# Decode attention on one core: explicit semaphores, hardware loops on TensorE, and A's loads ahead of B's

## The chip, the cores and the metric

The kernel runs on one core of one Trainium2 chip. Times are device microseconds (us) of that core, as medians of several executions. On a single core the runs carry no visible slow state; all runs compared here were marked "fast", and their times lie within about 0.4% of each other for any one kernel. A change counts as faster or slower when it moves the time by over 2%.

Names of engines in profile lines: PE is TensorE (PEld its weight loads), DVE VectorE, ACT ScalarE, POOL GpSimd, and SPq the SyncE queue that issues the DMAs. The page counts 16 DMA engines for the core.

## The reference, cut to what matters

Two single-token decode attentions, A and B, each with 32 heads of 128. A reads 16384 keys and values per head, B only the last 4096. Weights `wq` and `wo` are 4.2 MB each, for each problem.

```python
q = (x @ wq).reshape(B, Sq, Hq, Dh)                      # one token
scores = einsum("bhqd,bhkd->bhqk", q, k) * Dh ** -0.5
o = einsum("bhqk,bhkd->bhqd", softmax(scores), v)
out = o.reshape(B, Sq, Hq * Dh) @ wo
# A: k, v = k_cache, v_cache;  B: the last 4096 keys of each head;  result: concat(A, B)
```

K and V alone are 335.5 MB (A 2 x 134.2 MB, B 2 x 33.6 MB). Everything is read from HBM once (the page: 352.32 MB read).

## The kernel before

K and V come in 20 "loads" (16 of A, 4 of B) of 256 keys on each of 128 partitions: 8.39 MB for k and as much for v. There are two buffers for k (`kt`) and one for v (`vt`). For each load, VectorE multiplies k by q, adds the two halves of the 128 columns, TensorE sums the remaining 64 columns into PSUM (32 matmuls against an identity, the "bank sums"), VectorE reduces the last 8 values, ScalarE takes the exponential, and TensorE multiplies by v ("p.v", 64 matmuls). VectorE then picks the useful quarter of the result, and TensorE folds it into the heads' sums. An A load is one unit of two heads. A B load is two units of four heads, each with its own two halves of the DMA.

The main loop, written for a framework that places the semaphores itself:

```python
loads = []                                  # A A A A B  A A A A B ...
per = len(stA.loads) // len(stB.loads)
for i, x in enumerate(stA.loads):
    loads.append(x)
    if i % per == per - 1:
        loads.append(stB.loads[i // per])
...
for i, x in enumerate(loads):
    n = KEYS // (4, 2)[i] if i < 2 else KEYS
    for k in range(0, KEYS, n):
        _mult(nc, cx, x, k, k + n)                 # DVE, k *= q
        if prev is not None and k == 0:
            _softmax(nc, cx, prev)                 # DVE reduce, ACT exp
        _add(nc, cx, x, k, k + n)                  # DVE
        if prev is not None and k == 0:
            for u in prev.units:
                _pv(nc, cx, u)                     # PE, frees the v buffer
        _red(nc, cx, x, k, k + n)                  # PE bank sums, frees a k buffer
    if prev is not None:
        end(prev)                                  # DVE pick, PE fold
    prev = x
```

All of it is unrolled: TensorE's program has more than 4,000 instructions (the page counts 2148 matmuls and 2148 weight loads). The DMA queue gets k(i+1), then v(i), then k(i+2), and so on; v(i) may be issued when p.v of load i-1 is done, and k(i+2) when the bank sums of load i are done.

The softmax here doesn't subtract the row's maximum and nothing guards it: scores larger than these inputs give would overflow.

## Time and profile before

| | before |
|---|---|
| time, median | 823.2 us |
| span in the profile | 821.2 us |
| data moved by the main queue | 352.33 MB |
| busy share of that queue | 99.3% |
| DVE / PE / ACT busy | 73% / 37% / 4% |

From the page of the kernel before: two rows of the 40 equal slices of the span (busy tenths of the DMA engines, and what they moved), and the table of DMA queues (packets, MB, share of the 16 engines' time).

```profile
DMA  9999999999999999999999999999999999999997
GB/s 383 434 457 412 456 412 454 412 454 418 427 442 444 425 441 429 441 416 447 421 445 437 431 435 434 432 423 443 441 418 451 425 445 421 448 413 455 413 424 317
q1 hardware_dynamic: 8212, 352.33, 99.3%
q8 instruction: 16, 0.26, 0.1%
```

The DMA engines are busy in every slice. The swing between 412 and 457 GB/s is only a matter of counting: packets count where they start, and in a slice (20.5 us) an engine starts 8 or 9 packets of 64 KB (2.42 us each). Neighbouring slices average about 434. q8 is the fetching of TensorE's own program, 16 blocks of 16 KB.

One steady period, from the timeline of the kernel before (start us, us, engine, line, operation, result and operands, count, and in brackets the idle time before and what ended it):

```profile
294.62 17.23 DVE L169 TENSOR_TENSOR kt<-kt,qallA 128x32768 bf16<-128x32768 bf16 x1 [9.23 <-DMA kt<-in_A_k_cache_dram]
...
313.96 8.68 DVE L178 TENSOR_TENSOR kt<-kt 128x16384 bf16<-128x16384 bf16 x1
...
315.23 5.97 PE L231 MATMUL acc<-vt,p_sb 128*8 128x512 bf16 x64 [23.70 <-ACT p_sb L212]
...
321.25 0.53 SPq L158 DMA_DIRECT2D vt<-in_A_v_cache_dram  x1
...
322.70 7.08 PE L190 MATMUL red<-kt,ident 128*128 128x512 bf16 x32 [1.51 <-DVE kt L178]
...
329.71 0.41 PE L259 MATMUL f_ps<-s,selA 128*32 128x128 f32 x2
329.81 1.18 SPq L158 DMA_DIRECT2D kt<-in_B_k_cache_dram  x2
333.27 17.23 DVE L169 TENSOR_TENSOR kt<-kt,qallA 128x32768 bf16<-128x32768 bf16 x1 [9.29 <-DMA kt<-in_A_k_cache_dram]
```

Read it from the DMA queue's side. A multiply starts when its k has landed, so k loads land at 294.6 and 333.3, 38.7 us apart. The next v load was handed to the queue at 321.25, 12 us before the k load ahead of it was done. That "lead" is what keeps the queue from running empty.

The end of the span, from the same kernel's timeline:

```profile
815.69 1.04 PE L307 MATMUL out_ps<-wo_t,ocB 128*1 128x256 bf16 x16 [0.43 <-DMA wo_t<-in_B_wo_dram]
...
816.91 1.00 PE L307 MATMUL out_ps<-wo_t,ocB 128*1 128x256 bf16 x12 [0.18 <-DMA wo_t<-in_B_wo_dram]
...
818.21 0.38 PE L307 MATMUL out_ps<-wo_t,ocB 128*1 128x256 bf16 x4 [0.29 <-DMA wo_t<-in_B_wo_dram]
```

TensorE waits for each of the last pieces of B's `wo`, but only for 0.2 to 0.4 us.

### The profile page before, as it was taken

How to read it: one execution, taken by the hardware profiler on the slowest of the kernel's cores; microseconds unless marked ns; L12 is line 12 of the kernel's file. 1: busy time of each engine (PE TensorE's matmuls, PEld its weight loads, DVE VectorE, ACT ScalarE, POOL GpSimd, SP SyncE). 2: the span in 40 equal slices, each digit the busy share in tenths (PEclk: the TensorE clock that was granted, in tenths of full speed). 3: DMA queues.
4: the chain of work that ended last, by engine and by line, in shares of the span. 5: the costliest groups of instructions: out<-in, count | busy, mean ns of one | idle time of the engine just before them, and what ended most of it. 6: DMA issues, size and time to landing. Idle time of an engine off the chain costs nothing.

```text
span 821.2 us, 4767 instructions
## 1 busy us (share of the span) xinstructions
PE 301.1 (37%) x2148; PEld 117.3 (14%) x2148; DVE 600.7 (73%) x146; ACT 35.1 (4%) x133; POOL 1.3 (0%) x9
## 2 busy tenths in 40 slices
PE   3433705143223415060606151423414250606076
PEld 1111202011011102020202020101101020202033
DVE  2099895997496867799196949599659677689921
ACT  0100000000010000000001000000001000000010
POOL 0000000000000000000000000000000000000000
PEclk9855668586767677675858585857666676768599
DMA  9999999999999999999999999999999999999997
GB/s 383 434 457 412 456 412 454 412 454 418 427 442 444 425 441 429 441 416 447 421 445 437 431 435 434 432 423 443 441 418 451 425 445 421 448 413 455 413 424 317
DMA packets 8235, 352.62 MB, mean 429 GB/s; under 512 B 916, under 2 KB 920, under 8 KB 1304
## 3 DMA queue, kind: packets, MB, share of 16 engines
q1 hardware_dynamic: 8212, 352.33, 99.3%
q8 instruction: 16, 0.26, 0.1%
q14 instruction: 3, 0.02, 0.0%
q10 hardware_dynamic: 4, 0.00, 0.0%
HBM read 352.32 MB, written 0.00 MB: 429 GB/s over the span
## 4 chain that ended last, share of the span: by engine, by line
DMA 61%; issue 15%; DVE 13%; PE 11%; ACT 0%; SPq 0%; DVEq 0%
DMA kt<-in_A_k_cache_dram 42%; DMA vt<-in_A_v_cache_dram 12%; PE red L190 7%; DVE kt L178 6%; DVE kt L169 4%; PE acc L231 4%; DMA vt<-in_B_v_cache_dram 4%; DMA wo_t<-in_B_wo_dram 4%; DVE sc L206 2%; ACT p_sb L212 0%; SPq L115 0%; PE out_ps L307 0%; DVE rowB L316 0%; DVEq L169 0%
## 5 line engine op out<-in xcount | busy, mean ns | idle before, releaser
L169 DVE TENSOR_TENSOR kt<-kt,qallA 128x32768 bf16<-128x32768 bf16 (+2 forms) x20 | 276.2, 13810 | 162.5 <-DMA kt<-in_A_k_cache_dram 162.5
L231 PE MATMUL acc<-vt,p_sb 128*8 128x512 bf16 (+1 forms) x1280 | 113.0, 530 | 444.4 <-ACT p_sb L212 344.4
L178 DVE TENSOR_TENSOR kt<-kt 128x16384 bf16<-128x16384 bf16 (+2 forms) x24 | 174.3, 7261 | 0.2
L190 PE MATMUL red<-kt,ident 128*128 128x512 bf16 x640 | 151.2, 396 | 54.6 <-DVE kt L178 54.6
L231 PEld LDWEIGHTS <-p_sb 128*8 128x8 bf16 (+1 forms) x1280 | 37.6, 112 | 515.7 <-ACT p_sb L212 419.8
L190 PEld LDWEIGHTS <-ident 128*128 128x128 bf16 x640 | 63.0, 101 | 142.2 <-issue 47.1
L169 DVE TENSOR_TENSOR kt<-kt,qallB 128x16384 bf16<-128x16384 bf16 x8 | 69.5, 8686 | 2.9 <-DMA kt<-in_B_k_cache_dram 2.9
L206 DVE TENSOR_REDUCE sc<-red 128x256 f32<-128x2048 f32 x20 | 45.7, 2284 | 5.6 <-PE red L190 5.6
L212 ACT ACTIVATE p_sb<-sc,offA 128x256 bf16<-128x256 f32 x32 | 16.0, 500 | 574.7 <-DVE sc L206 574.7
L245 DVE TENSOR_TENSOR acc<-acc,maskA 128x512 f32<-128x512 f32 x16 | 11.1, 694 | 21.4 <-PE acc L231 21.4
L212 ACT ACTIVATE p_sb<-sc,offB 128x128 bf16<-128x128 f32 x32 | 12.4, 388 | 161.2 <-DVE sc L206 161.2
L130 PE MATMUL q_ps<-wq_t,scr 128*128 128x512 bf16 x64 | 15.7, 407 | 6.9 <-DMA wq_t<-in_A_wq_dram 4.9
L251 DVE TENSOR_REDUCE s<-acc 128x128 f32<-128x512 f32 x24 | 16.6, 691 | 0.8
L307 PE MATMUL out_ps<-wo_t,ocA 128*1 128x512 bf16 x32 | 8.8, 443 | 0.3 <-DVE ocA L300 0.3
L245 DVE TENSOR_TENSOR acc<-acc,maskB 128x512 f32<-128x512 f32 x8 | 5.5, 692 | 4.5 <-PE acc L231 4.5
L130 PEld LDWEIGHTS <-scr 128*128 128x128 bf16 x64 | 6.5, 103 | 15.6 <-issue 8.0
L316 DVE CAST rowA<-out_ps 1x512 bf16<-1x512 f32 x1 | 0.7, 678 | 8.8 <-PE out_ps L307 8.8
L259 PE MATMUL f_ps<-s,selA 128*32 128x128 f32 x32 | 6.5, 285 | 0.0
L212 ACT ACTIVATION_READ_ACCUMULATOR p_sb<-sc,offA 128x1 f32 x32 | 6.0, 187 | 0.0
L212 ACT ACTIVATION_READ_ACCUMULATOR p_sb<-sc,offB 128x1 f32 x32 | 6.0, 186 | 0.0
L307 PE MATMUL out_ps<-wo_t,ocB 128*1 128x256 bf16 x64 | 4.3, 272 | 1.8 <-DMA wo_t<-in_B_wo_dram 0.9
L102 DVE CAST scr<-xT 128x128 bf16<-128x128 f32 (+1 forms) x6 | 2.1, 459 | 3.6 <-PE xT L94 3.5
(43 smaller groups left out, 26.4 us busy)
## 6 DMA issues: line engine op xcount, KB each, us to landing
kt<-in_B_k_cache_dram SPq DMA_DIRECT2D x8, 4096.0 KB, 32.4
vt<-in_B_v_cache_dram SPq DMA_DIRECT2D x8, 4096.0 KB, 23.8
wq_t<-in_A_wq_dram SPq DMA_DIRECT2D x1, 4096.0 KB, 12.2
wq_t<-in_B_wq_dram SPq DMA_DIRECT2D x1, 4096.0 KB
wo_t<-in_A_wo_dram SPq DMA_DIRECT2D x2, 2048.0 KB, 22.6
wo_t<-in_B_wo_dram SPq DMA_DIRECT2D x1, 2048.0 KB, 27.0
wo_t<-in_B_wo_dram SPq DMA_DIRECT2D x1, 1024.0 KB, 29.0
wo_t<-in_B_wo_dram SPq DMA_DIRECT2D x1, 512.0 KB
```

The lines of the kernel that those rows point to most:

```text
L102: cx.o(nc.vector.tensor_copy(st.xb[:, :, g, :].rearrange("p c (i r) -> p r c i", r=R)[:, g, :, :], xT[:, :].rearrange("p (c o) -> p c o", ...
L130: cx.o(nc.tensor.matmul(q_ps[:, j, :], lhsT=st.xb[:, c, g, :], rhs=w[:, g, j * (512 // DH) : (j + 1) * (512 // DH), :], start=(g == 0 and ...
L169: cx.o(nc.vector.tensor_tensor(out=k, in0=k, in1=q.rearrange("p (o d) -> p o d", o=1).broadcast_to([P, b - a, DH]), op=ALU.mult,))
L178: cx.o(nc.vector.tensor_tensor(out=k[:, :, 0 : DH // 2], in0=k[:, :, 0 : DH // 2], in1=k[:, :, DH // 2 : DH], op=ALU.add,))
L190: cx.o(nc.tensor.matmul(load.red[:, k : k + n, :], lhsT=cx.ident[:, :], rhs=load.kt[:, k : k + n, b * W : (b + 1) * W], start=(b == 0), st ...
L206: cx.o(nc.vector.tensor_reduce(out=sc[:, :], in_=load.red[:, :, :], axis=AX.X, op=ALU.add))
L212: cx.o(nc.scalar.activation(out=u.p[:, :, g, :], in_=sc[:, u.k0 : u.k0 + n].rearrange("p (t e) -> p t e", e=4), func=ACT.Exp, scale=SCALE, ...
L231: cx.o(nc.tensor.matmul(u.acc[r : r + 4 * R, :], lhsT=u.p[:, t, :, :], rhs=u.load.vt[:, k : k + 4, :], start=(t < 4), stop=(t >= T - 4),))
L245: cx.o(nc.vector.tensor_tensor(out=acc, in0=acc, in1=st.mask[:, :].rearrange("p (x o) -> p x o", o=1).broadcast_to([P, 4, DH]), op=ALU.mult,))
L251: cx.o(nc.vector.tensor_reduce(out=u.s[:, :], in_=acc.rearrange("p x d -> p d x"), axis=AX.X, op=ALU.add,))
L259: cx.o(nc.tensor.matmul(cx.f_ps[st.f_at : st.f_at + 32, 0:DH], lhsT=st.sel[:, at : at + 32], rhs=u.s[:, :], start=(u.i == 0), stop=(u.i == ...
L307: cx.o(nc.tensor.matmul(out[x], lhsT=st.oc[:, j : j + 1], rhs=st.wo_t[:, j, x * w : (x + 1) * w], start=(j == 0), stop=(j == J - 1),))
```

## The change

Its intent: replace the framework's automatic synchronisation by semaphores set by hand, so that TensorE can run two hardware loops (16 turns over A's loads, 3 over B's, one load left over), each with an inner loop over the four PSUM banks of the sums. A loop over one kind of load needs A's loads in a row, so all of A precedes B. The order on TensorE becomes sums(i), p.v(i), fold(i), sums(i+1): the fold, which waits for VectorE's pick, now stands ahead of the next sums. Before, it came after them. The core of the diff:

```diff
-    loads = []
-    per = len(stA.loads) // len(stB.loads)
-    ...                                          # A A A A B
+    loads = [stA] * stA.L + [stB] * stB.L
...
+    def take(self, eng, n=1):                    # class _Sem
+        eng.wait_ge(self.h, n)
+        eng.sem_inc(self.h, -n)
...
+    def red(slot):
+        with e.Fori(0, NB) as n:
+            cx.s_add.take(e)
+            for b in range(W):
+                ins = mm(
+                    cx.red[:, bass.ds(n, 1), :], lhsT=cx.ident[:, :],
+                    rhs=banks[:, bass.ds(slot * NB + n, 1), :, b * W : (b + 1) * W],
+                    start=(b == 0), stop=(b == W - 1),
+                )
+            ins.then_inc(cx.s_red.h, 1)
+    def pv(st, vt, sems):
+        for u in range(st.U):
+            cx.s_p.take(e)
+            sems[u].take(e, 16)
+            ...                                  # the matmuls, unrolled as before
+            ins.then_inc(cx.s_pv.h, 1)
+        for u in range(st.U):
+            cx.s_pick.take(e)
+            ins = mm(cx.f[...], lhsT=cx.win[u][:, :], rhs=cx.s[u][:, :], start=False, stop=True)
...
+    loop = lambda a, b: nc.Fori(a, b, engines=cx.pe_only, head_slot={PE: 0})
+    with loop(1, 1 + stA.L) as i:
+        red(i % 2)
+        pv(stA, cx.vt, cx.s_v)
+    norm(stA)
+    with loop(1 + stA.L, len(loads)) as i:
+        red(i % 2)
+        pv(stB, cx.vt, cx.s_v)
+    red(n % 2)
+    pv(stB, cx.kt[:, _slot(n - 2), :, :], cx.s_vlast)
+    norm(stB)
```

The DMA queue's program keeps the same transfers in the same pattern (k ahead, v behind), each behind a hand-written wait on `s_red` or `s_pv`.

## The prediction

> What bounds the kernel now: the DMA queue. On the page, the data queue moved 352.33 MB and was busy 99.3% of the 821.2 us span, and the DMA row of the slices shows 9 in all but the last. The table by stretch of time shows 431 to 435 GB/s in every stretch from 42 to 785 us. [...] DVE is busy 73%, PE 37%, ACT 4%.
>
> Steady period of one A load, from the timeline at 294.6 to 333.3 us: 38.7 us for 16.8 MB. In it DVE works 17.2 (multiply) + 2.3 (reduce) + 8.7 (add) + 1.4 (pick) = 29.6 us; PE works 6.0 (p.v) + 7.1 (bank sums) + 0.4 (fold). The next v load is issued when p.v ends (321.25), 12 us before the k load ahead of it in the queue has landed (333.3). The k load after that is issued when the bank sums end (329.8), over 20 us before its turn. So compute can slip 12 us per load before the queue runs dry.
>
> What the change does:
> - Order on PE: the fold of load i now precedes the bank sums of i+1, which therefore wait for the pick: from 322.7 to about 324.7, 2 us later. Slack 20 us: worth 0.
> - Loops: register work, branches, explicit waits. [...] inside the slack: 0.
> - Instruction fetch: 0.26 MB now; perhaps 0.2 MB goes, 0.5 us at 429 GB/s.
> - A before B: same bytes, same transfers. DVE per B load is 17.4 + 2.3 + 8.7 + 2.8 = 31 us, below 38.7, so B loads in a row stay DMA-bound.
> - Start: the first k load lands at 42 us, q is ready at about 32; 10 us to spare. [...]
> - Tail: the last weight piece lands at 818.2; PE waits 0.2 to 0.4 us for each of the last pieces, so has about 1.3 us to spare. The load before the last is now a B load of two units, so its p.v ends near 781 instead of 785.3, which pays for the later pick[...]. End still set by DMA: 0 to +2 us.
>
> Sum: nothing of size lies on the critical path. I predict 822.5 us (before 823.2), range 819.0 to 826.5; faster by over 2%: 0.01, within 2%: 0.96, slower by over 2%: 0.03.
>
> What would show it: data queue still about 99% busy at 428 to 431 GB/s; instruction-queue bytes below 0.1 MB; bank sums starting about 2 us after the adds end; v loads issued over 8 us before the k load ahead lands; last p.v done before 803; last step of the chain a weight-load DMA, then under 1 us of PE.
>
> What would make it wrong: [...] a gap in the queue from the new k-load waits; B loads in a row streaming at another rate than A's.

The forecast came to 822.5 us, 0.7 below the 823.2 before. Terms of it are cut here, because nothing measured stood behind them: an allowance per load for the loops, counted as 0 and again hidden in the tail, and up to 1 us for entering the explicit section. The terms left are -0.5 us for the instruction bytes and 0 to +2 us at the tail.

## The result, and the profile after

| | before | after |
|---|---|---|
| time, median | 823.2 us | 822.4 us |
| span in the profile | 821.2 us | 820.4 us |
| instruction blocks for TensorE | 16 (0.26 MB) | 4 (0.07 MB) |
| bank sums, busy in total | 151.2 us | 183.3 us |
| main queue's busy share | 99.3% | 99.3% |

The ratio is 0.9987, with a 95% interval of 0.997 to 1.0005. Ratios here and below are the mean time of one kernel's runs over that of the other's of the same rounds, so they are not quite the ratio of the medians quoted.

The same lines of the page, kernel after:

```profile
DMA  9999999999999999999999999999999999999997
q1 hardware_dynamic: 8212, 352.33, 99.3%
q8 instruction: 4, 0.07, 0.0%
```

One steady period of the kernel after, from its timeline:

```profile
294.82 17.23 DVE L292 TENSOR_TENSOR kt<-kt,qallA 128x32768 bf16<-128x32768 bf16 x1 [9.23 <-DMA kt<-in_A_k_cache_dram]
...
314.16 8.68 DVE L300 TENSOR_TENSOR kt<-kt 128x16384 bf16<-128x16384 bf16 x1
...
315.67 5.89 PE L364 MATMUL acc<-vt,p 128*8 128x512 bf16 x64 [20.39 <-PEq L42]
321.60 0.53 SPq L150 DMA_DIRECT2D vt<-in_A_v_cache_dram  x1
...
323.57 0.69 DVE L327 TENSOR_REDUCE s<-acc 128x128 f32<-128x512 f32 x1
324.41 0.60 PE L364 MATMUL f<-s,win 128*32 128x128 f32 x2 [2.85 <-PEq L42]
325.58 9.50 PE L364 MATMUL red<-kt,ident 128*128 x32 [0.57 <-PEq L42]
333.42 17.23 DVE L292 TENSOR_TENSOR kt<-kt,qallA 128x32768 bf16<-128x32768 bf16 x1 [9.15 <-DMA kt<-in_A_k_cache_dram]
335.12 0.54 SPq L150 DMA_DIRECT2D kt<-in_A_k_cache_dram  x1
```

The fold now stands ahead of the sums. The sums begin 2.7 us after the add ends (at 322.8) and take 9.5 instead of 7.1 us, so the next k load is issued 5.3 us later (335.1 against 329.8). And yet the k loads land 38.6 us apart, as before: the v load is still handed over 11.8 us ahead of its turn, and the k load issued at 335.1 stands behind a v transfer that has only just begun. "PEq L42" names the wait instruction in the helper; it is TensorE's own sequencer waiting on a semaphore.

The end of the kernel after:

```profile
815.87 1.01 PE L364 MATMUL red<-vt,ocB 128*1 128x256 bf16 x12 [0.15 <-DMA vt<-in_B_wo_dram]
817.13 0.38 PE L364 MATMUL red<-vt,ocB 128*1 128x256 bf16 x4 [0.25 <-DMA vt<-in_B_wo_dram]
```

DMA still ends last, but only 0.4 us of waiting are left in these lines.

A warning on the chain of waits: the page's chain of the kernel before spread its time over many DMAs, engines and lines; that of the kernel after covers only the last 4% of the span.

```profile
DMA 4%; PE 0%; SPq 0%; DVE 0%; issue 0%
```

It starts at 778.4 us. A chain this short says nothing about the 95% in front of it; the DMA rows and the lead do.

### The profile page after: what moved, and what is told of

Same layout as the page of the kernel before. It is cut to its first block, busy times and chain, and to the rows that moved or that the text cites. A ratio compares the mean times of both kernels' runs of the same rounds, so it can differ in the third digit from the quotient of the medians. Undisturbed runs are those within 1.5% of the kernel's fastest.

```text
span 820.4 us, 5948 instructions
## 1 busy us (share of the span) xinstructions
PE 338.6 (41%) x2149; PEld 128.4 (16%) x2149; DVE 603.5 (74%) x172; ACT 35.5 (4%) x134; POOL 1.3 (0%) x9
## 3 DMA queue, kind: packets, MB, share of 16 engines
q1 hardware_dynamic: 8212, 352.33, 99.3%
## 5 line engine op out<-in xcount | busy, mean ns | idle before, releaser
L292 DVE TENSOR_TENSOR kt<-kt,qallA 128x32768 bf16<-128x32768 bf16 (+2 forms) x20 | 276.2, 13810 | 155.8 <-DMA kt<-in_A_k_cache_dram 155.8
L364 PE MATMUL acc<-vt,p 128*8 128x512 bf16 (+1 forms) x1216 | 111.1, 543 | 353.4 <-PEq L42 353.4
L364 PE MATMUL red<-kt,ident 128*128 x640 | 183.3, 456 | 43.3 <-PEq L42 43.3
L364 PEld LDWEIGHTS acc<-vt,p 128*8 128x8 bf16 (+1 forms) x1216 | 36.8, 113 | 427.1 <-issue 419.3
L364 PEld LDWEIGHTS red<-kt,ident 128*128 128x128 bf16 x640 | 72.5, 113 | 150.4 <-issue 103.7
L216 ACT ACTIVATE p<-sc,offA 128x256 bf16<-128x256 f32 x32 | 16.0, 500 | 604.9 <-DVE sc L306 604.9
L364 PE MATMUL f<-s,win 128*32 128x128 f32 x48 | 11.0, 317 | 61.4 <-PEq L42 61.4
L364 PE MATMUL red<-vt,kt 128*128 128x512 bf16 x64 | 15.6, 406 | 8.0 <-DMA vt<-in_A_wq_dram 5.9
L216 ACT ACTIVATE p<-sc,offB 128x128 bf16<-128x128 f32 x32 | 12.4, 388 | 115.7 <-DVE sc L306 115.7
L327 DVE TENSOR_REDUCE s<-acc 128x128 f32<-128x512 f32 x24 | 16.6, 692 | 0.8
L364 PEld LDWEIGHTS red<-vt,kt 128*128 128x128 bf16 x64 | 6.5, 103 | 16.7 <-issue 10.4
L364 PE MATMUL red<-vt,ocA 128*1 128x512 bf16 x32 | 8.5, 433 | 0.0
## 6 DMA issues: line engine op xcount, KB each, us to landing
vt<-in_B_wo_dram SPq DMA_DIRECT2D x1, 2048.0 KB, 29.6
```

What stands on the lines that cost most here:

```text
L216: ins = e.activation(out=p[:, :, g, :], in_=cx.sc[:, u * st.keys : (u + 1) * st.keys].rearrange("p (t e) -> p t e", e=4), func=ACT.Exp, sc ...
L292: n = did(e.tensor_tensor(out=k, in0=k, in1=q.rearrange("p (o d) -> p o d", o=1).broadcast_to([P, b - a, DH]), op=ALU.mult,))
L327: cx.s_pick.on(e.tensor_reduce(out=cx.s[u][:, :], in_=acc.rearrange("p x d -> p d x"), axis=AX.X, op=ALU.add,))
L364: mm = lambda *a, **k: e.matmul(*a, skip_group_check=True, **k)
```

## The experiments

The theory: the DMA queue sets the time; compute has about 12 us of lead per load and next to none at the end; what differs between the kernels is the instruction traffic and the two ends. Rivals are stated with each run.

### The three parts of the change, one at a time

`before_a_first` is the kernel before with only the order changed. `unrolled` is the kernel after with TensorE's loops written out. `after_again` is the kernel after itself. The three ran on one chip, five rounds each.

```diff
 # before_a_first
-    loads = []
-    ...
+    loads = stA.loads + stB.loads
 # unrolled
-        with e.Fori(0, NB) as n:
+        for n in range(NB):
-    with loop(1, 1 + stA.L) as i:
+    for i in range(1, 1 + stA.L):
-    with loop(1 + stA.L, len(loads)) as i:
+    for i in range(1 + stA.L, len(loads)):
```

> The changed kernel unaltered, for a tight interval beside the other two of this call. Theory (queue-bound, only 0.19 MB of instruction bytes and the two ends differ): 0.5 to 1.3 us faster than before, ratio 0.9985 to 0.9995. Rival (nothing differs, the 0.8 us is scatter between chips): ratio 1.000 within 0.0005.

> The changed kernel with the tensor engine's loops written out: explicit semaphores and A before B stay, hardware loops go. Theory: instruction bytes return to about 0.26 MB, the 32 bank sums of a load return from 9.5 to about 7.1 us, the next k load is issued 2 to 3 us earlier, and the time rises by the instruction bytes alone, about 0.5 us, so about 822.8. Rival 1 (loop overhead costs time): faster than the changed kernel by more than 1 us. Rival 2 (the gain comes from explicit semaphores or the order, not the loops): same as the changed kernel within 0.2 us.

> The kernel before with one edit, all of A's loads ahead of B's. Theory: same bytes through a full queue, so the time is that of before within 0.4 us (ratio 0.9995 to 1.0005); the product of p and v of the load before the last ends about 4 us earlier, hidden. Rival (order is what moved the end 1 us earlier): about 822.2, ratio 0.9985 to 0.999.

| kernel | order | semaphores | loops | median us (lowest to highest) | ratio to before |
|---|---|---|---|---|---|
| before | A A A A B | automatic | no | 823.21 (822.87 to 823.55) | 1 |
| before_a_first | A first | automatic | no | 823.31 (822.94 to 823.66) | 1.0001 |
| unrolled | A first | explicit | no | 824.93 (824.45 to 824.99) | 1.002 |
| after_again | A first | explicit | yes | 822.63 (822.39 to 822.88) | 0.9993 |

The order alone is worth nothing (+0.1 us). The rewrite with explicit semaphores, still unrolled, costs 1.6 us. The loops give 2.3 us back. So the small net change is two opposite changes, each larger than the sum, and my expectation of 0.5 us for the loops was too small by a factor of over four. The net gain itself (0.6 us here, 0.8 us in the first measurement) is as expected, and the ranges of the two kernels overlap by 0.01 us at most; but the intervals of both ratios include 1, so by them a gain of zero isn't ruled out.

In the unrolled kernel's timeline around 325 us the sums take 8.5 us against 7.1 before and 9.5 after:

```profile
324.41 0.59 PE L364 MATMUL f<-s,win 128*32 128x128 f32 x2 [2.49 <-PEq L42]
324.93 8.51 PE L364 MATMUL red<-kt,ident 128*128 128x512 bf16 x32
```

Their total of busy time over the run is 171.5 us against 151.2 and 183.3. So most of what the sums got slower (20 of 32 us) came without any loop. The pause ahead of them is longer too (2.5 us before the fold, against 1.5 us before), but no run changed the pause by itself, so it is not shown to be the reason. What the traces do show is a lower clock. The view by windows over just these 32 matmuls (tile `ident`), for the kernels before, unrolled and after; the third number from the right is the granted clock:

```profile
322.70:329.78 7.08, 7.08 (x32) 3.05 (x32) 0.00 (x0) 0.00 (x0) 1.00 1.02 444
324.93:333.44 8.51, 8.51 (x32) 3.39 (x32) 0.00 (x0) 0.00 (x0) 0.83 0.96 416
325.58:335.08 9.50, 9.50 (x32) 3.73 (x32) 0.00 (x0) 0.00 (x0) 0.74 1.02 442
```

Time multiplied by clock is 7.0 to 7.1 us in all three. In these groups a matmul starts either 0.43 or 0.22 us after the one ahead of it. In the traces of the kernels before and after, all 208 steps of 0.40 to 0.45 us fall where the record of the granted clock stands at 0.5, and all 985 of 0.20 to 0.23 us where it stands at 1.0. Over the whole run 39, 136 and 191 of the 640 sums have the slow step, and at 0.21 us each that is the 20 and the 12 us. So the loops' 12 us, too, are accounted for by these slow steps, a lower clock and not slower issue. None of this reached the time: the kernel with the slowest sums is the fastest of the four.

Where do 2.3 us come from, then? The page of the unrolled kernel:

```profile
q1 hardware_dynamic: 8212, 352.33, 99.1%
q8 instruction: 17, 0.28, 0.1%
```

Thirteen more blocks of 16 KB are 0.21 MB, or 0.5 us at 432 GB/s (the kernel before moved 431 to 435 from 42 to 785 us). The bytes don't explain it. The packets in the trace do better. Worked out from the start and length of every packet of 2 KB or more on the main queue: the last moment (us, looked at every 0.1 us) at which at least n packets were in flight on the 16 engines.

```
                blocks fetched   n=16    n=12    n=8     n=4     n=2     n=1
after                 4          814.8   814.9   815.2   816.3   816.6   816.7
before               16          814.7   815.2   817.5   817.7   817.8   817.8
before_a_first       16          814.6   814.9   817.5   817.6   817.7   818.0
unrolled             17          814.9   815.2   817.7   817.9   818.3   819.1
```

(A 17th block of `before_a_first` came at 822.6 us, after the end of the span.)

In all four kernels some engines run out of work at about 815 us. In those that fetch 16 or 17 blocks, eight packets are still in flight at 817.5 us; in the kernel after, the last of all ends at 816.7. In the trace a block's own packet takes about 0.94 us (mean), while a 64 KB data packet takes 2.42 us. The reading that fits: a fetch takes the place of data on one engine, fetches fall on half of the engines, and the time is that of the last engine, not of the mean. The next two runs put this to the test.

### More instruction blocks

`pv_x2` (below) runs p.v twice in a small hardware loop and takes 822.34 us. `pv_x2_unrolled` is the same arithmetic with every loop written out. `pool_fill` leaves TensorE as in the kernel after and gives the idle POOL engine a long useless program.

```diff
 # pv_x2_unrolled: as unrolled, and
-                with e.Fori(0, rep) as _:
+                for _ in range(rep):
                     once()
 # pool_fill, at the end of POOL's program
+    cx.s_pool.wait(e, 2)
+    for turn in range(8):
+        for i in range(1024):
+            ins = e.memset(cx.scratch[:, i : i + 1], 0)
+        cx.s_own.wait(e, cx.s_own.on(ins))
```

> pv_x2 with every tensor-engine loop written out: same arithmetic as pv_x2 (822.34 us), some 27 instead of 4 instruction blocks fetched. Theory (fetches delay single DMA engines): slower than pv_x2 by more than the 2.3 us that 13 more blocks cost the unrolled kernel, 825 to 829 us, with a wider spread of the engines' ends. Rival 1 (bytes only, 0.4 MB): 823.3. Rival 2 (unrolled code as such costs 2.3 us, whatever its length): 824.6.

> The changed kernel with 8192 useless one-column fills at the end of the otherwise idle POOL engine's program[...] while the tensor engine's loops and all data transfers stay as they are. Theory (fetches pass through the same 16 DMA engines and each delays the one that carries it by about 0.95 us, so that engines end unevenly): the last data packets of the 16 engines end over more than the 2 us of the changed kernel, 825 to 835 us. Rival 1 (only the bytes count, 0.53 MB at 432 GB/s): 823.6. Rival 2 (the unrolled kernel was slower because of the tensor engine's own timing): 822.4.

(The page below has 64 packets more on q14 than the kernel after, 0.52 MB.)

`pv_x2_unrolled`: 826.43 us (826.19 to 826.54), 27 blocks. Against `pv_x2`, measured in another call, that is 4.1 us for 23 more blocks, 0.18 us each. Against that, `unrolled` minus `after_again` is 2.3 us for 13 blocks, also 0.18 us each. A block's bytes at 432 GB/s would be 0.04 us. Its packets show the two halves again: 16 in flight until 814.6 us, 8 until 819.0, the last until 820.6. Both rivals (823.3 by bytes, 824.6 by "unrolled code as such") fell.

The kept traces show the rest of the mechanism. On one engine the next packet starts 3 or 4 ns before a 64 KB packet ends, so the packets can be chained into 16 rows, one for each engine (rows that end a packet in the same nanosecond can be swapped). In `pv_x2_unrolled` the first 16 fetches fall on eight of the rows, twice over in the same order; the other eight rows get none of them. A fetch takes 0.88 to 0.98 us, and a 64 KB packet behind it 2.9 to 3.0 instead of 2.42 us (in the kernel before 0.88 to 1.00 and 2.9 to 3.0): together about 1.4 us on its engine. Over eight engines that is 0.18 us per block, the cost that both pairs gave.

The cost comes in steps, because the last engine counts. The engines end near 815.0, 816.6, 817.8, 819.2 and 820.5 us, each step about one block's 1.4 us. With 4 blocks (`after`) four engines end on the second step. With 16 (`before`, `before_a_first`) eight end on the third. With 17 (`unrolled`) seven end on the third and one on the fourth. With 26 before 819 us (`pv_x2_unrolled`) six end on the fourth and two on the fifth. This is what blocks dealt out in turn to eight engines give. So most of the 1.6 us of "explicit semaphores" is probably the 17th block and not the waits; no run changed one without the other.

`pool_fill`: 863.97 us, ratio 1.0496, far above the 825 to 835 that I expected. Its page:

```profile
q1 hardware_dynamic: 8212, 352.33, 95.5%
q14 instruction: 67, 0.55, 0.2%
```

POOL's program came in 64 blocks of 8 KB, one every 5.5 us, and while it ran the A period was 43.9 instead of 38.7 us: 5.2 us for eight blocks, 0.65 us each, and 64 x 0.65 = 41.6 us is the whole loss. The queue's share over the whole run fell to 95.5%, and single slices to 299 GB/s. Chaining the packets as above shows why: from 228 to 353 us all 22 of POOL's fetches fall on one and the same row. Each takes 0.31 us and makes the data packet behind it 0.35 us longer, 0.66 us together. That engine has no gap in this stretch, while the other fifteen are busy for only 90 or 91% of it: every transfer waits for the one engine. The 8192 fills that POOL wrote meanwhile are a rival that no run removed, and 2 or 3 of some 46 packets on each other engine were slow as well; but those engines had time to spare. So the fetches are enough to account for the loss (0.5 MB that no one waits for cost 41 us).

### How much lead there is

`pv_x2`, `pv_x3` and `pv_x4` run every p.v but the last load's two, three and four times in a small loop. The sum restarts each time, so the result is the same. The v load is issued later, and nothing else changes.

```diff
-            for t in range(T):
-                ...
-            ins.then_inc(cx.s_pv.h, 1)
+            with e.Fori(0, rep) as _:
+                once()                           # the matmuls and their semaphore
...
-        cx.s_pv.wait(e, pv)
+        cx.s_pv.wait(e, REP * pv)
```

> Each product of p and v but the last load's is run twice (same result, restarted sum), in a small hardware loop: about 6 us more tensor-engine work per load, 115 us in all, before the next v load may be issued. Theory: an A load's period is the longer of 38.7 us (the queue) and 21.4 us (a v load on an otherwise empty queue, 19.4 plus about 2 to start and land) plus the product's own time. 21.4 + 11.8 = 33.2, so the time stays at 822 to 824; v loads are issued about 6 instead of 12 us before the k load ahead lands. Rival (work shown in the chain of waits adds up: bank sums 7%, product 4%): about 100 us slower.

The "about 2 to start and land" can be read in the kernel before: `wq` of A, the first load on an empty queue, landed 12.2 us after its issue (page, part 6), of which its 4.19 MB at 432 GB/s are 9.7; that leaves 2.5 us.

> As pv_x2, three times: 21.4 + 17.7 = 39.1 us plus loop turns, just over 38.7. Theory: the edge; 0.4 to 1.5 us on each of 16 A loads, 825 to 845 us. B loads have two units that overlap load and product, so they don't slow. Rival (the tensor engine, busy only 40%, has room to spare until it is near full): same time, 822.

> As pv_x2, four times: 21.4 + 23.6 = 45 us plus loop turns, about 6.3 to 8 us over the queue's 38.7 on each A load. Theory: 915 to 950 us, with the queue's busy share down near 88%, the tensor engine still idle a third of the time. Rival (room until the tensor engine is full; it would be about 75% busy): same time.

| kernel | median us | ratio | p.v of an A load, us | lead of v issue, us | mean A period, us | granted clock |
|---|---|---|---|---|---|---|
| after | 822.4 | 0.9987 | 4.9 to 6.5 | 11.2 to 12.9 | 38.63 | 0.695 |
| pv_x2 | 822.34 | 0.9986 | 8.4 to 9.7 | 7.9 to 10.2 | 38.68 | 0.756 |
| pv_x3 | 824.07 | 1.0002 | 11.8 to 13.3 | 4.2 to 5.8 | 38.77 | 0.798 |
| pv_x4 | 850.96 | 1.0327 | 15.4 to 16.6 | 1.4 to 3.8 | 39.66 | 0.827 |

The lead is read as in the period above: the start of the next multiply minus the issue of the v load. The period is the mean of the 13 between A's third load and its last. Adding 3 us per load costs nothing, adding 6 to 7 us little (1.7 us in all), adding 10 us breaks through. That is the slack of some 12 us, minus about 4 us which a load seems to need as a head start. In `pv_x4`, from the timelines of SPq and DVE:

```profile
380.06 0.54 SPq L151 DMA_DIRECT2D vt<-in_A_v_cache_dram  x1
```

```profile
380.89 0.69 DVE L328 TENSOR_REDUCE s<-acc 128x128 f32<-128x512 f32 x1
381.53 17.23 DVE L293 TENSOR_TENSOR kt<-kt,qallA 128x32768 bf16<-128x32768 bf16 x1
```

Here the v load was handed over only 1.5 us before the multiply of the next k began, and the queue's share over the run fell to 96.7%.

My expectations for x3 and x4 missed in size (825 to 845, 915 to 950), and for one reason: I priced each repeat at the 5.9 us of the first, and it cost 3.3. The granted clock of the run rose with the repeats, from 0.695 to 0.827, while TensorE's busy time in the stretch from 100 to 600 us rose from 202.5 to 297.3 us. In the profiled execution `pv_x4` is 29.9 us longer. Its last data packet comes 19.2 us later (835.9 against 816.7), 13 us of it in these 13 periods of 1.0 us more. The other 10.7 us are the end: after the last data packet it took 14.4 us to the end of the span (835.9 to 850.3), against 3.7 in the kernel after.

### The end of the kernel

`tail_red_x2` repeats the bank sums of the last load only.

```diff
-            for b in range(W):
+            for b in list(range(W)) * rep:
...
-    red(n % 2)
+    red(n % 2, 2)
```

> Only the bank sums of the last load are done twice (same result): about 8 us more tensor-engine work once, after the last k load. Theory: at the end the tensor engine waits for weight pieces 0.15 and 0.25 us only, so of 8 us about 0.4 to 1 is hidden: 829 to 830.5 us, and the last wait for a weight piece is gone. Rival (the end is set by the DMA with room to spare, as in the middle): 822.

It took 826.81 us (825.91 to 827.24), 4.4 us more than the kernel after and less than the 829 to 830.5 that I expected. The timeline shows how 6.8 us shrank to that: the sums went from 8.76 to 15.59 us, but the first 29 output matmuls that follow ran faster, 6.42 instead of 7.86 us, and the 0.4 us of waiting for weight pieces went too.

```profile
784.39 15.59 PE L364 MATMUL red<-kt,ident 128*128 x64
...
812.56 6.42 PE L364 MATMUL red<-vt,ocA 128*1 128x512 bf16 x29
...
819.26 3.00 PE L364 MATMUL red<-vt,ocB 128*1 128x256 bf16 x52
```

The last group has no bracket any more: TensorE no longer waits for DMA at the end. So extra TensorE work of 3 us on each of the first 19 loads was free (`pv_x2`), and on the 20th most of it was paid.

### Less vector work, fewer bytes

`thin_dve` lets the multiply and the add touch 16 of 128 columns. `half_v` moves half of each v load. Both compute something else.

```diff
 # thin_dve
-            k = cx.kt[:, _slot(i), a:b, :]
+            k = cx.kt[:, _slot(i), a:b, 0:16]
 ...                                              # q and the add likewise
 # half_v
+            if which == "v":
+                out, src = out[:, 0 : st.keys // 2, :], src[:, :, 0 : st.keys // 2, :]
```

> Wrong result on purpose: the multiply and the add of each load touch 16 of 128 columns only, so vector-engine work falls from about 600 to under 200 us while every DMA stays. Theory: queue-bound, 820 to 823 us; idle time of the vector engine grows by what it was spared. Rival (vector work on the chain of waits, 13%, counts): tens of us faster. Rival 2 (vector traffic on the on-chip memory slows the loads): steady rate rises above 435 GB/s and the time falls by over 2 us.

> Wrong result on purpose: only half of each v load is moved, 352.3 to 268.4 MB. Theory: the queue's period per load falls to about 29 us, just under the vector engine's 29.6 (A) and 31 (B), so that engine takes over: 38.7 falls to about 30 per load, 820 to about 650 us (640 to 670), vector engine about 92% busy, queue no longer full. Rival (bytes alone): 268.4 MB at 432 GB/s plus the ends, 628 us.

`thin_dve`: 822.47 us, ratio 0.9988. Removing 446 us of the vector engine's 603 us changed nothing. What the multiply no longer does, the engine waits:

```profile
L292 DVE TENSOR_TENSOR kt<-kt,qallA 128x4096 bf16<-128x4096 bf16 (+2 forms) x20 | 37.3, 1864 | 217.4 <-DMA kt<-in_A_k_cache_dram 217.4
```

In the kernel after this group is busy for 276.2 us and idle ahead of it for 155.8. The comparison with the reference accepted this kernel although its scores are wrong, so with these inputs acceptance says little about the scores.

`half_v`: 694.73 us, ratio 0.843. Fewer bytes do move the time, which no other edit did by such an amount. The rival (bytes alone, 628 us) fell, and the expected 640 to 670 was missed too. From its table of the stretch from 100 to 600 us (busy us of each engine, then clock, DMA share and GB/s):

```profile
100.00:600.00 500.00, 235.91 (x1580) 89.84 (x1581) 474.25 (x105) 19.94 (x77) 0.00 (x0) 0.75 0.95 400
```

VectorE is busy for 474 of 500 us. The mean A period is 31.3 us, against 29.6 us of vector work: the next limit stands right behind the queue, as expected. The rest of the miss is at the two ends, which I had let shrink along with the loads. At the end, 17 us pass from the last data packet to the end of the span.

### A body longer than one block

`pair_body` runs A's loop 8 times over two loads, so the body holds over 300 instructions. A block holds fewer: the 4296 instructions that the page of the kernel before counts on TensorE, in 16 blocks, are about 270 each (an estimate).

```diff
-    with loop(1, 1 + stA.L) as i:
-        red(i % 2)
-        pv(stA, cx.vt, cx.s_v)
+    with loop(0, stA.L // 2) as i:
+        for s in (1, 0):
+            red(s)
+            pv(stA, cx.vt, cx.s_v)
```

> A's loop runs 8 times over two loads instead of 16 times over one: the body grows from some 170 to over 300 instructions[...]. Theory: if the block left behind is no longer held, each turn fetches it again (instruction bytes up from 0.07 MB by up to 0.26 MB)[...]; inside the slack, so 822 to 823.5 us. [...]

(The theory's "if" is what the run asks; its 0.26 MB are 16 blocks of 16 KB, two for each of the 8 turns.)

822.47 us, ratio 0.9988, and no block was fetched anew on each turn: five blocks in all for the 8 turns and the rest of the program, one more than in the kernel after.

```profile
q8 instruction: 5, 0.08, 0.0%
```

No refetch occurred at this length, so the experiment can't tell what one would cost.

No version was found that beats both kernels by more than the scatter. In its middle the kernel after already moves 428 to 439 GB/s in every stretch of 100 us, and all of the 352.33 MB are needed once.

## Why the prediction was right

- "What bounds the kernel now: the DMA queue." Right. `thin_dve` took 446 us of vector work away for nothing; `half_v` took 24% of the bytes and the time fell by 16%, until VectorE was the limit.
- "Compute can slip 12 us per load before the queue runs dry." Right in kind, but the usable slack is nearer 8 us, because a load needs a head start: a lead of 4 to 6 us cost 1.7 us in all, one of 1.4 to 3.8 us cost 1.0 us per load.
- "Bank sums starting about 2 us after the adds end": 2.7 us in the period shown. For the loops, "inside the slack: 0": the sums took 2.4 us longer there, but the unrolled kernel shows that more than half of this came without loops, and the granted clock accounts for all of it. Worth 0, as said.
- "Instruction fetch: ... 0.5 us." The direction was right; the term was mis-sized. The loops are worth 2.3 us, because a fetched block costs 0.18 us of the end on average and not the 0.04 us of its bytes. I had priced its bytes over all 16 engines; but a block held one engine for 1.4 us, only eight engines carried such blocks, and the last engine counted.
- The step to explicit semaphores cost 1.6 us as a whole, more than was allowed and probably for another reason. In the profiles, 0.2 us of it is the later first load (1.02 against 0.80 us). The last data packet is 1.1 us later than in `before_a_first`, on one engine alone. The 17th block of the unrolled kernel is fetched at 811 us, inside the last transfers, and that of the other at 822.6 us, after them; the steps found above fit this, but no run tested it by itself. The rest, 0.3 us, comes after the last data packet. The predicted net (0.7 us) was met within 0.1 us because this cost and the loops' larger gain nearly cancel, which is luck.
- "A before B": worth 0.1 us, as said.
- "Tail ... End still set by DMA." Right, with 0.4 us to spare and not the 1.3 that I had read; `tail_red_x2` shows that more would not have been hidden.
- "What would make it wrong": neither of the risks there came. The queue had no gap (428 GB/s or more in every stretch of 100 us from 100 to 700), and B's k loads landed 38.7 us apart, as A's did. Four instruction blocks were fetched in all, and v loads kept a lead of over 11 us. The predicted instruction bytes below 0.1 MB (0.07), last p.v before 803 us (802.5), and v loads issued over 8 us ahead all held.

## What to carry to other kernels

When one queue is full, ask of each change only how late it makes the next issue, and compare that with the lead of that issue over its turn; here 3 us per load were free in the middle and 6 to 7 us nearly so, while at the end of the kernel TensorE had only 0.4 us of waiting left. The small differences of this DMA-bound kernel were set by the last of the DMA engines, so instruction traffic cost several times its bytes: rolling TensorE's program into loops was worth 2.3 us though the bank sums took 183.3 us with the loops against 171.5 without, and a long program on an idle engine cost 41 us. When a rewrite comes out even, build the versions between: here a gain and a loss of about 2 us stood behind a net of 0.7.
